# Query projection with x as the fixed operand and wq moving in 512 columns, in a one-token attention and MLP kernel

## Chip, cores, metric

One core of one Trainium2 chip (eight cores on two dies). The metric is the device time of one execution in microseconds, taken as the median of several runs. A profiled execution's span (first to last instruction) is about 1.9 us shorter than its time.

## The reference, cut to what matters

Two batch rows of one token, width 448. After a layer norm, 16 query heads of 256 attend to the last 4096 positions of 8 key and value heads, and an MLP runs beside it; all three are summed.

```python
q = (xn @ wq)                      # [2,448] @ [448,4096]
k, v = k_cache[:, :, Sk - 4096:], v_cache[:, :, Sk - 4096:]   # 2 x 8 heads x 4096 x 256, bf16
o = softmax(q k^T / 16) v
out = x + o @ wo + mish_mlp(xn)    # w1 448x1792, w2 1792x448
```

k and v are 33.6 MB each, the weights 10.6 MB (wq, wo 3.67 each, w1 and w2 together 3.21): 77.7 MB must be read for 2 x 448 outputs.

One warning about correctness: with inputs this small the softmax is nearly flat, and the comparison with the reference passes even when the query is a constant. So the comparison does not prove that the new projection gives the right q.

## The kernel before

wq borrows one of two large buffers that later hold v. It lies there as 128 partitions x 7 slices x 2048 columns. The projection uses 128x128 blocks of wq as the fixed operand and x (4 columns) as the moving one. The result has to be copied four times along the partitions ("spread").

```python
wq_sb = v_tile()[:, 0 : NS * HW].rearrange("p (s n) -> p s n", s=NS)   # 1 of 2 v buffers
nc.sync.dma_start(out=wq_sb, in_=A_wq...)                              # 28 KB runs
...
def project():
    for hh in range(HH):
        for e in range(NE):
            for s in range(NS):                                        # 8 * 2 * 7 = 112
                nc.tensor.matmul(qT_ps[:, hh, e, :], lhsT=wq_v[:, s, hh, e, :],
                                 rhs=xs[:, s, :, :]..., start=(s == 0), stop=(s == NS - 1))
    nc.vector.tensor_copy(out=qT[:], in_=qT_ps...)
    for b4 in range(NB):                                               # 4 spread matmuls
        nc.tensor.matmul(qr_ps[:, b4, :], lhsT=spread[:, b4, :], rhs=qT[:], ...)
    nc.vector.tensor_copy(out=qrep..., in_=qr_ps[:])
# build_q(i): eight GpSimd copies qrep -> qdiag[i % 2], the fixed operand of the scores
# ... cut ...
load_k(0); load_dense(); project(); build_q(0); build_q(1); turn(0)    # turn: DVE transpose of k
for i in range(Hkv + 1):
    load_k(i + 1); load_v(i); load_wo(i)      # all on one DMA queue, in this order
    # per quarter: turn, scores (PE), exp (ACT), transpose of p (DVE)
    # then the MLP (once, i == 0), values(i - 1), output of head i - 2
```

k and v have two buffers each. A load is issued when the last reader of its buffer is done, so the issue times of the loads are where a slower engine could reach the DMA stream.

The softmax here doesn't subtract the row's maximum and nothing guards it: scores larger than these inputs give would overflow.

## Time and profile before

| | before |
|---|---|
| time, median of the first 3 runs | 190.34 us (190.32 to 190.46) |
| span of the profiled run | 188.4 us |
| read from HBM | 77.67 MB |
| rate from 60 to 100, and 100 to 140 us | 429, 430 GB/s |
| PE busy in those 80 us | 66.6 us (83%) |
| DVE busy in those 80 us | 48.2 us (60%) |

The rate is the same in both 40 us stretches, whatever the engines do; PE is the busiest engine and still has a sixth of its time free.

### The profile page before, as it was taken

To read this page: it belongs to the slowest core of one execution; us is meant where nothing else is said; L and a number is where in the kernel's file an instruction comes from. 1 tells how busy PE (TensorE), PEld (TensorE's weight loads), DVE (VectorE), ACT (ScalarE), POOL (GpSimd) and SP (SyncE) were. 2 spreads that over 40 slices of the span, in tenths; PEclk is the share of its full clock that TensorE was granted. 3 is DMA by queue.
4 is the path that set the end of the run, shared out by engine and by line. 5 is a ranking of instruction groups with operands and counts; after the bars stand their busy time and mean duration, and the time that the engine had idled before them with its cause. 6 is when DMAs were issued, how large, how long until landed. Compare 5 with 4: busy or idle time off the path is not lost.

```text
span 188.4 us, 2773 instructions
## 1 busy us (share of the span) xinstructions
PE 138.5 (74%) x1118; PEld 68.2 (36%) x1118; DVE 106.0 (56%) x155; ACT 41.4 (22%) x140; POOL 16.1 (9%) x74
## 2 busy tenths in 40 slices
PE   0143079935989679966996599947996699988963
PEld 0042023733434234423342234413442334433852
DVE  6901299059931993089704991099606993967201
ACT  3100004400440315012421224012421224124101
POOL 6004200300030002100030003000030000000000
PEclk9999999955999978999799969995899969999855
DMA  6999899999999999999999999999999999999990
GB/s 226 445 444 428 383 432 438 445 442 440 431 431 438 445 407 404 433 438 398 462 447 431 431 431 438 414 418 420 449 431 431 412 423 435 473 418 386 427 375 23
DMA packets 5509, 77.82 MB, mean 413 GB/s; under 512 B 501, under 2 KB 2553, under 8 KB 2938
## 3 DMA queue, kind: packets, MB, share of 16 engines
q1 hardware_dynamic: 5492, 77.66, 96.8%
q8 instruction: 8, 0.13, 0.2%
q14 instruction: 3, 0.02, 0.0%
q10 hardware_dynamic: 6, 0.01, 0.0%
HBM read 77.67 MB, written 0.00 MB: 412 GB/s over the span
## 4 chain that ended last, share of the span: by engine, by line
DMA 67%; DVE 18%; PE 11%; ACT 1%; SPq 0%; issue 0%; ACTq 0%; DVEq 0%
DMA k<-in_A_k_cache_dram 58%; DVE kt L377 14%; DMA v<-in_A_v_cache_dram 10%; PE sc L389 6%; PE o L448 4%; DVE pT L415 3%; PE q L498 1%; PE psA L225 1%; ACT p L403 1%; DVE oT L462 0%; DVE sums L424 0%; SPq L353 0%; DVE osum L483 0%; SPq L111 0%; ACTq L595 0%
## 5 line engine op out<-in xcount | busy, mean ns | idle before, releaser
L377 DVE STREAM_TRANSPOSE kt<-k 128x2048 f32<-128x2048 f32 x32 | 73.1, 2289 | 57.0 <-DMA k<-in_A_k_cache_dram 57.0
L389 PE MATMUL sc<-kt,qdiag 128*128 128x512 bf16 x256 | 71.1, 437 | 19.7 <-DVE kt L377 19.6
L403 ACT ACTIVATE p<-sc,off 128x256 bf16<-128x256 f32 x64 | 33.0, 544 | 84.2 <-PE sc L389 83.5
L389 PEld LDWEIGHTS <-qdiag 128*128 128x128 bf16 x256 | 26.3, 107 | 61.1 <-issue 35.6
L448 PE MATMUL o<-v,pT 128*8 128x512 bf16 x192 | 42.5, 379 | 0.0
L448 PEld LDWEIGHTS <-pT 128*8 128x8 bf16 x192 | 17.2, 92 | 22.4
L272 POOL COPY qdiag<-qrep 32x16 bf16<-32x16 bf16 x64 | 13.0, 247 | 121.8 <-PE sc L389 107.4
L415 DVE STREAM_TRANSPOSE pT<-p 128x512 bf16<-128x512 bf16 x32 | 21.6, 677 | 2.8 <-ACT p L403 2.8
L403 ACT ACTIVATION_READ_ACCUMULATOR p<-sc,off 128x1 f32 x64 | 11.7, 183 | 0.0
L456 ACT COPY o_sb<-o 8x512 f32<-8x512 f32 x6 | 3.4, 574 | 36.3 <-PE o L448 36.3
L225 PE MATMUL psA<-wo,oT 128*2 128x112 bf16 x128 | 3.6, 238 | 8.9 <-DVE oT L462 8.9
L498 PE MATMUL q<-pT,v 128*128 128x4 bf16 x256 | 7.4, 168 | 1.9 <-DMA v<-in_A_v_cache_dram 1.8
L498 PEld LDWEIGHTS <-v 128*128 128x128 bf16 x256 | 7.2, 100 | 2.1 <-DMA v<-in_A_v_cache_dram 1.9
L246 PE MATMUL qT_ps<-xs,v 128*128 128x4 bf16 x112 | 3.1, 166 | 6.0 <-DMA v<-in_A_wq_dram 6.0
L225 PEld LDWEIGHTS <-oT 128*2 128x2 bf16 x128 | 1.8, 87 | 9.8 <-DVE oT L462 9.6
L246 PEld LDWEIGHTS <-v 128*128 128x128 bf16 x112 | 3.1, 104 | 6.2 <-DMA v<-in_A_wq_dram 6.2
L225 PE MATMUL psA<-v,act_bf 128*2 128x112 bf16 x56 | 1.5, 296 | 5.0 <-DVE act_bf L335 5.0
L188 PE MATMUL xnT_ps<-ident,xn_bf 2*128 2x2 bf16 x7 | 0.5, 167 | 5.4 <-DVE xn_bf L138 5.4
L479 PEld LDWEIGHTS q<-ident_f,o_sb 8*128 8x128 f32 x24 | 3.3, 206 | 3.0 <-issue 3.0
L462 DVE TENSOR_TENSOR oT<-q,rec 128x8 bf16<-128x8 f32 x2 | 0.3, 167 | 6.9 <-PE q L498 6.9
L479 PE MATMUL q<-ident_f,o_sb 8*128 8x8 f32 x24 | 3.8, 264 | 0.0
L303 PE MATMUL hT_ps<-xs,v 128*128 128x4 bf16 x49 | 3.7, 195 | 0.0
(55 smaller groups left out, 39.7 us busy)
## 6 DMA issues: line engine op xcount, KB each, us to landing
k<-in_A_k_cache_dram SPq DMA_DIRECT2D x7, 4096.0 KB, 29.7
v<-in_A_v_cache_dram SPq DMA_DIRECT2D x7, 4096.0 KB, 30.1
k<-in_A_k_cache_dram SPq DMA_DIRECT2D x2, 2048.0 KB
v<-in_A_wq_dram SPq DMA_DIRECT2D x1, 3584.0 KB
v<-in_B_w_dram SPq DMA_DIRECT2D x2, 1568.0 KB, 25.9
wo<-in_A_wo_dram SPq DMA_DIRECT2D x7, 448.0 KB, 29.7
v<-in_A_v_cache_dram SPq DMA_DIRECT2D x1, 2048.0 KB, 15.0
v<-in_A_v_cache_dram SPq DMA_DIRECT2D x1, 1536.0 KB, 18.1
```

The lines of the kernel that those rows point to most:

```text
L225: nc.tensor.matmul(part(n), lhsT=lhsT, rhs=w[:, n * DO : (n + 1) * DO], start=start, stop=stop, tile_position=(0, n * Q), skip_group_check ...
L246: nc.tensor.matmul(qT_ps[:, hh, e, :], lhsT=wq_v[:, s, hh, e, :], rhs=xs[:, s, :, :].rearrange("p x b -> p (x b)"), start=(s == 0), stop=( ...
L272: nc.gpsimd.tensor_copy(out=tv[rows, :, e, j * Q : (j + 1) * Q : HS].rearrange("p n (b h) -> p n b h", b=Bsz), in_=qrep[rows, :, h0 : h0 + ...
L303: nc.tensor.matmul(hT_ps[:, c, :, :].rearrange("p x b -> p (x b)"), lhsT=w1_v[:, s, c, :], rhs=xs[:, s, :, :].rearrange("p x b -> p (x b)" ...
L377: nc.vector.transpose(out=kt[:].bitcast(FP32), in_=k[:, half * TH * Dh : (half + 1) * TH * Dh].bitcast(FP32),)
L389: nc.tensor.matmul(psc[:], lhsT=qdiag[i % NW][:, n * NE + e, :], rhs=ktv[:, n, e, :, :], start=(n == 0 and e == 0), stop=(n == NB - 1 and ...
L403: nc.scalar.activation(out=pv[:, b, :, :], in_=sv[:, b, :, :], func=ACT.Exp, scale=scale, bias=off[:, b : b + 1], accum_out=state["rs", i] ...
L415: nc.vector.transpose(out=pT[:], in_=p_t.pop(s)[:])
L448: nc.tensor.matmul(po[:], lhsT=pT_t[i * NH + piece][:, uh * NP * Q : (uh + 1) * NP * Q : HS], rhs=v[:, u * NP : (u + 1) * NP, :].rearrange ...
L456: nc.scalar.copy(out=o_sb[:], in_=po[:])
L479: nc.tensor.transpose(pqv[:, u, c, :], ov[:, u, c, :], ident_f[0:NR, 0:NR])
L498: nc.tensor.matmul(po[:, c, :], lhsT=vv[:, t, c, :], rhs=pTv[:, th, 0:Q:HS], start=(t == 0 and c == 0), stop=(t == T - 1), skip_group_chec ...
```

## The change

The intent: x becomes the fixed operand (already repeated in four groups of 32 columns, so the spread step falls away), wq streams through in 512 columns, 28 matmuls in place of 112 and 4, and wq comes in two loads, so that PE can start after the first four of seven slices. A 32x32 transpose on DVE then puts q on the partitions.

```diff
-    nc.sync.dma_start(out=wq_sb, in_=A_wq...)
+    SC = NS // 2 + 1
+    for lo, hi in ((0, SC), (SC, NS)):
+        nc.sync.dma_start(out=wq_sb[:, lo:hi, :], in_=wq_in[:, lo:hi, :])
...
-    spread = consts.tile([P, NB, P], BF16)        # memset and 16 small DVE copies
...
     def project():
-        (112 matmuls wq x xs, cast, 4 spread matmuls, cast to qrep)
+        nc.vector.tensor_copy(out=xq[:, :, :, 0:NXB], in_=xs...to_broadcast([P, NS, NQ, NXB]))
+        pools = (ps_sc, "sc"), (ps_sc, "sc"), (ps_o, "o"), (ps_o, "o")
+        ps = [pool.tile([P, N5], FP32, tag=tag, name="q_ps") for pool, tag in pools]
+        for s in range(NS):
+            for u in range(4):
+                nc.tensor.matmul(ps[u][:], lhsT=xq[:, s, :, :]..., 
+                                 rhs=wq_sb[:, s, u * N5 : (u + 1) * N5], ...)
+        for u in range(4):                        # DVE, ACT, DVE, ACT
+            copy(out=q_sb[:, u * N5 : (u + 1) * N5], in_=ps[u][:])
+        nc.vector.transpose(out=qt[:].bitcast(FP32), in_=q_sb[:, 0:HW].bitcast(FP32))
...
     # build_q reads qt instead of qrep
```

More of the change, by code (lines that the diff above doesn't have):

```diff
@@ L110 @@
     wq_sb = v_tile()[:, 0 : NS * HW].rearrange("p (s n) -> p s n", s=NS)
-    nc.sync.dma_start(
-        out=wq_sb,
-        in_=A_wq.rearrange("r (x n) -> (r x) n", x=NX).rearrange("(p s) n -> p s n", s=NS),
-    )
+    wq_in = A_wq.rearrange("r (x n) -> (r x) n", x=NX).rearrange("(p s) n -> p s n", s=NS)
+    SC = NS // 2 + 1
+    for lo, hi in ((0, SC), (SC, NS)):
+        nc.sync.dma_start(out=wq_sb[:, lo:hi, :], in_=wq_in[:, lo:hi, :])
     make_identity(nc, ident[:])
@@ L149 @@
         )
-    spread = consts.tile([P, NB, P], BF16)
-    nc.gpsimd.memset(spread[:], 0.0)
-    for b4 in range(NB):
-        rows = slice(b4 * Q, (b4 + 1) * Q)
-        for j in range(NQ):
-            nc.vector.tensor_copy(
-                out=spread[rows, b4, j * Q : (j + 1) * Q], in_=ident[rows, rows]
-            )
     hsel = hsel[:, 0:BR]
@@ L235 @@
     add(ident[0:Bsz, 0:Bsz], x_bf[:, :], start=True)
-    qrep = consts.tile([P, NB, HH, NE, NX, Bsz], BF16)
-    wq_v = wq_sb.rearrange("p s (h m e) -> p s h e m", h=HH, e=NE)
-    def project():
-        qT_ps = ps_m.tile([P, HH, NE, NX * Bsz], FP32, tag="m", name="qT_ps")
-        for hh in range(HH):
-            for e in range(NE):
-                for s in range(NS):
-                    nc.tensor.matmul(
-                        qT_ps[:, hh, e, :],
-                        lhsT=wq_v[:, s, hh, e, :],
-                        rhs=xs[:, s, :, :].rearrange("p x b -> p (x b)"),
-                        start=(s == 0),
-                        stop=(s == NS - 1),
-                    )
-        n = HH * NE * NX * Bsz
-        qT = consts.tile([P, n], BF16, name="qT")
-        nc.vector.tensor_copy(out=qT[:], in_=qT_ps[:].rearrange("p h e c -> p (h e c)"))
-        qr_ps = ps_m.tile([P, NB, n], FP32, tag="m", name="qr_ps")
-        for b4 in range(NB):
-            nc.tensor.matmul(
-                qr_ps[:, b4, :], lhsT=spread[:, b4, :], rhs=qT[:], start=True, stop=True
-            )
+    xq = consts.tile([P, NS, NQ, Q], BF16)
@@ L261, in project @@
+    nc.gpsimd.memset(xq[:], 0.0)
+    NXB = NX * Bsz
+    qt = consts.tile([P, HW], BF16)
+    qv = qt[:].rearrange("p (h n k e) -> p n h k e", h=HH, n=NB, e=NE)
+    def project():
         nc.vector.tensor_copy(
-            out=qrep[:].rearrange("p n h e x b -> p n (h e x b)"), in_=qr_ps[:]
-        )
+            out=xq[:, :, :, 0:NXB],
+            in_=xs[:].rearrange("p s x b -> p s (x b)").unsqueeze(2).to_broadcast([P, NS, NQ, NXB]),
+        )
+        N5 = HW // 4
+        pools = (ps_sc, "sc"), (ps_sc, "sc"), (ps_o, "o"), (ps_o, "o")
+        ps = [pool.tile([P, N5], FP32, tag=tag, name="q_ps") for pool, tag in pools]
+        for s in range(NS):
+            for u in range(4):
+                nc.tensor.matmul(
+                    ps[u][:],
+                    lhsT=xq[:, s, :, :].rearrange("p j k -> p (j k)"),
+                    rhs=wq_sb[:, s, u * N5 : (u + 1) * N5],
+                    start=(s == 0),
+                    stop=(s == NS - 1),
+                )
+        q_sb = kt_pool.tile([P, TH * Dh], BF16, tag="kt", name="q_sb")
+        for u in range(4):
+            copy = nc.vector.tensor_copy if u % 2 == 0 else nc.scalar.copy
+            copy(out=q_sb[:, u * N5 : (u + 1) * N5], in_=ps[u][:])
+        nc.vector.transpose(out=qt[:].bitcast(FP32), in_=q_sb[:, 0:HW].bitcast(FP32))
@@ L275, in build_q @@
                     ),
-                    in_=qrep[rows, :, h0 : h0 + rep, e, x, :].rearrange("p n h b -> p n b h"),
+                    in_=qv[rows, :, h0 : h0 + rep, x * Bsz : (x + 1) * Bsz, e].rearrange(
+                        "p n h b -> p n b h"
+                    ),
                 )
```

## The prediction

> **What bounds the kernel now.** I read the page's busy shares first, then the chain that ended last, the DMA rows in 40 slices, the queue of DMA issues in order of time, the first 36 us in order of time, and the busy time and GB/s in short windows.
>
> Busy shares: PE 74%, DVE 56%, ACT 22%, POOL 9%. The DMA rows say something else (each digit is the mean busy share of the 16 DMA engines in 1/40 of the span, 4.71 us; below it the rate):
>
> ```profile
> DMA  6999899999999999999999999999999999999990
> GB/s 226 445 444 428 383 432 438 445 442 440 431 431 438 445 407 404 433 438 398 462 447 431 431 431 438 414 418 420 449 431 431 412 423 435 473 418 386 427 375 23
> DMA packets 5509, 77.82 MB, mean 413 GB/s; under 512 B 501, under 2 KB 2553, under 8 KB 2938
> ...
> DMA 67%; DVE 18%; PE 11%; ACT 1%; SPq 0%; issue 0%; ACTq 0%; DVEq 0%
> ```
>
> From the second slice to the last but one the transfers never pause. The first slice moved 226 x 4.71 = 1.06 MB, some 2.4 us worth, so they start at about 2.3 us; the last data of v release PE at 182.75 us. 77.7 MB in 180.4 us is 431 GB/s. So the time is a head of 2.3 us, a stream of 180.4 us and a tail of 188.4 - 182.75 = 5.7 us. The stream is the bound. The chain's 67% for DMA understates it: where the chain passes through DVE or PE (as at 22.5 to 32.5 us, before the issue of the third k load) the rows above show that the DMA engines were busy with earlier loads.
>
> The projection lies in the head (start us, us, engine, line, operation):
>
> ```profile
> 5.42 1.61 DVE L155 COPY spread<-ident 32x32 bf16<-32x32 bf16 x16
> ...
> 12.09 3.15 PE L246 MATMUL qT_ps<-xs,v 128*128 128x4 bf16 x112 [6.03 <-DMA v<-in_A_wq_dram]
> ...
> 15.27 0.54 SPq L353 DMA_DIRECT2D v<-in_A_v_cache_dram  x1
> 15.27 0.22 DVE L255 CAST qT<-qT_ps 128x64 bf16<-128x64 f32 x1 [5.96 <-PE qT_ps L246]
> ...
> 15.96 0.42 DVE L261 CAST qrep<-qr_ps 128x256 bf16<-128x256 f32 x1 [0.46 <-PE qr_ps L258]
> 16.53 3.52 POOL L272 COPY qdiag<-qrep 32x16 bf16<-32x16 bf16 x16 [12.83 <-DVE qrep L261]
> ...
> 22.54 6.70 DVE L377 STREAM_TRANSPOSE kt<-k 128x2048 f32<-128x2048 f32 x3 [6.16 <-DMA k<-in_A_k_cache_dram]
> 24.90 9.92 PE L389 MATMUL sc<-kt,qdiag 128*128 128x512 bf16 x32 [8.98 <-DVE kt L377]
> ```
>
> PE waits until 12.09 for all of wq, projects in 3.15 us, and its end releases wq's buffer to the first v load (issued 15.27). The first block of qdiag is complete at 18.17 us (PE's first weight load from it), yet the scores start only at 24.90, because k lands at 22.54 and its transpose ends at 24.86. The query is thus ready almost 7 us early.
>
> How early the loads are issued, from the DMA queue in order of time:
>
> ```profile
> 2.96 0.55 SPq L353 DMA_DIRECT2D k<-in_A_k_cache_dram  x1
> 15.27 0.54 SPq L353 DMA_DIRECT2D v<-in_A_v_cache_dram  x1
> 15.85 0.60 SPq L370 DMA_DIRECT2D wo<-in_A_wo_dram  x1
> 32.55 0.54 SPq L353 DMA_DIRECT2D k<-in_A_k_cache_dram  x1
> 45.82 0.54 SPq L353 DMA_DIRECT2D v<-in_A_v_cache_dram  x1
> ```
>
> Bytes moved, summed from 5 us windows: 3.3 MB by 10 us, 7.8 by 20, 12.1 by 30, 14.2 by 35, 18.4 by 45, 22.8 by 55. Bytes submitted before the first v: wq 3.67 + k 4.19 + w1 and w2 3.21 + second k 4.19 = 15.27 MB, which the stream has used up at 37.5 us; so that v has 22 us to spare. The third k (issued 32.55) would be missed when 19.92 MB are through, at about 48.5 us: 16 us to spare. The second v (45.82) would be missed at 24.12 MB, about 58 us: 12 us to spare. Those are the three issues that a slower projection can push.
>
> **What the Trainium skill says.** "DMA: Bandwidth & Descriptors", Specifications, gives a fabric ceiling of 435 GB/s for the core's 16 engines; the trace's 431 GB/s over the stream agrees that there is nothing left to fill. The same table asks for runs of at least 512 B for line rate; wq's runs go from 28 KB to 16 and 12 KB, so I expect no loss (the trace has 28, 32 and 12.5 KB runs side by side at 428 to 445 GB/s). "Queues, rings and completion order" of that page says each engine consumes descriptors in ring order: the first piece of wq should land before the second, and neither later. "TensorE: Matmul & The Clock Gate", Part 1, says an idle array runs at half rate until some 3.4 us of sustained work, and gives 426.7 and 215.7 ns for 512 columns. The trace agrees in size: the first eight score matmuls take 3.59 us (449 ns each), their weight loads are 0.43 us apart from 24.91 to 30.41 us, and the 32 value matmuls at 54.8 us take 7.08 us (221 ns). The clock row reads full speed before 30 us although these matmuls are slow, so I trust durations there, not that row.
>
> **The change part by part.**
>
> Removed: 112 matmuls of 4 columns (3.15 us, 112 weight loads of 104 ns beside them), four spread matmuls (0.37), the casts qT and qrep (0.22 + 0.42), 16 small copies to spread (1.61 us of DVE before xs), and spread's memset (0.52 on POOL).
>
> Added: 28 matmuls of 512 columns; a broadcast copy xs to xq (estimate 0.25 us from the 0.22 us of the xs instructions); a memset of xq (128x896; the 128x1024 one takes 0.95, so 0.85 us, done by about 4 us on POOL); four evictions of 128x512, two on DVE and two on ACT; one DVE transpose of 128x1024 words; one more DMA issue (0.4 us of SP). In the order of instructions the loads, scores and transposes after the projection are unmoved; q's scratch takes one turn in the kt buffers, but the fifth k transpose still waits for the same scores.
>
> Start: xs was done at 9.3 us; without the spread copies 7.7, xq at 8.0. The first piece of wq is 2.10 MB, through at 5 + 0.81/0.402 = 7.0 us; all of wq was through at about 10.8 and released PE at 12.09, a lag of 1.3. So the first piece releases PE at 8.3 us, 3.8 us earlier.
>
> Matmuls: PE is cold. With 5.5 us of half rate as in the scores, some 13 cost 0.427 (to 13.8 us), the other 15 cost 0.221 (3.3 us): end at 17.2 us. If it stays cold, 28 x 0.427 = 12.0 us: end at 20.3. By then the second piece (12.1 us) has long landed, so PE doesn't wait for it. Compared with 15.24 the projection ends 2 to 5 us LATER in spite of its earlier start: its PE time grows from 3.15 to between 9 and 12 us.
>
> Behind it: evictions. The casts of 64 and 256 columns took 0.224 and 0.424 us, 1.04 ns a column, so 0.69 us for 512; two on DVE, of which the first starts 0.65 us before PE's end: done 0.75 us after it. ACT's 8x512 copy took 0.574, so ACT is done sooner. Transpose: half of the 2.29 us of 128x2048, 1.15 to 1.2 us. So qt stands 2.0 us after PE's end (before, qrep stood 1.14 us after): 19.2, or 22.3 cold. First qdiag, 8 x 0.22 = 1.76 us: 21.0, or 24.1.
>
> On the path: the scores wait for the k transpose, which starts at 22.54 with k's landing. DVE is free for it in both cases (19.2 or 22.3), and qdiag is there before 24.86. Change of the first scores, and of the third k issue: 0 us, at worst 0.5. The first v issue moves from 15.27 to between 17.3 and 20.4, against 37.5 that it may have. Stream: same bytes, same order; 128 more runs and one more completion, which I put at 0 to 0.2 us. Tail: untouched. Sum: 0 to +0.2 us on 190.34.
>
> **Rivals.**
> 1. The late projection starves the stream. For: PE work triples and q is later. Against: 12 to 22 us of backlog at each issue concerned, against a shift of at most 5. It would need q to be 10 us later than I reckon; then each further us costs one: 192 to 196.
> 2. The shorter projection path helps, as the change intends. For: PE starts 3.8 us earlier, and PE may be warm for the scores (cold matmuls there cost 14 x 0.21 = 3 us). Against: the k transpose waits for k's landing, which is the stream; earlier work can't bring bytes sooner. It would give 190.0 to 190.3 at best.
> 3. The split load changes the stream itself: smaller runs slower, or the dip at 19 to 24 us (383 GB/s) removed or made worse. A dip to 383 instead of 431 in one slice costs 0.5 us, so +-0.5: 189.8 to 190.9.
> 4. Another PE clock phase in the tail (64 matmuls in 1.87 us and 0.7 us for the output, at granted clock 0.50): a warm tail could take off up to about 1 us. The work from 165 us on is unchanged, so it should stay cold.
>
> **Range and chances.** The centre is 190.4. Rivals 3 and 4 and the scatter of before (0.14 us) give 189.7 to 191.1 for 8 in 10. The 2% bounds lie at 186.5 and 194.1. Faster needs less data, a faster stream than the 431 it has, or a tail shortened by two thirds: 0.01. Slower needs rival 1 or a broken stream: 0.03. Within 2%: 0.96.
>
> **What would show it.** Right: the mean of the DMA rows stays at 9 throughout with some 430 GB/s, the projection's first matmul at about 8.3 us and its last at 17 to 20.5, the first k transpose still at 22.5, scores at 24.9, the last v released at about 182.7, tail 5.7. PE busy grows by 5 to 9 us with no effect. Wrong: a slice of low DMA share between 35 and 60 us (rival 1), the first k transpose held back by qt rather than k's landing by more than 1 us, or a stream that ends at a clearly different time with the same bytes (rival 3).

## The result

| | before | changed |
|---|---|---|
| time, median of 6 runs each | 190.40 us (190.06 to 191.11) | 190.16 us (189.86 to 190.75) |
| ratio, 95% interval | | 0.9988 (0.9966 to 1.001): same |
| span of the profiled run | 188.4 us | 188.0 us |
| PE busy | 138.5 us | 140.3 us |
| rate from 60 to 100, and 100 to 140 us | 429, 430 GB/s | 429, 429 GB/s |

A ratio is the mean time of one kernel's runs over that of the other's of the same rounds, so it is not quite the ratio of the medians quoted.

The DMA rows of the changed kernel's page, and its chain by engine, answer to the first block of the prediction:

```profile
DMA  6999899999999999999999999999999999999991
GB/s 220 421 476 439 383 426 439 446 443 446 432 439 436 399 404 435 439 439 394 474 441 439 418 404 429 432 446 413 452 446 422 398 425 422 457 439 411 411 385 38
...
DMA 67%; DVE 19%; PE 11%; SPq 1%; ACT 1%; issue 0%; ACTq 0%; DVEq 0%
```

The same shape as before, down to the 383 in the fifth slice. That dip is thus not caused by the single wq load, and it is not removed by the split.

The changed kernel in order of time (start us, us, engine, line, operation, tiles, count, in brackets the idle time before and its releaser):

```profile
8.08 0.21 DVE L237 COPY xq<-xs 128x112 bf16<-128x112 bf16 x1
8.35 8.81 PE L246 MATMUL q_ps<-v,xq 128*128 128x512 bf16 x28 [1.97 <-DVE xq L237]
...
13.45 0.15 PEld L246 LDWEIGHTS <-xq 128*128 128x128 bf16 x1 [0.28 <-issue]
13.76 2.90 PEld L246 LDWEIGHTS <-xq 128*128 128x128 bf16 x14 [0.17 <-issue]
16.55 1.29 DVE L256 CAST q_sb<-q_ps 128x512 bf16<-128x512 f32 x2 [8.26 <-PE q_ps L246]
...
17.19 0.54 SPq L349 DMA_DIRECT2D v<-in_A_v_cache_dram  x1
...
17.94 1.25 DVE L257 STREAM_TRANSPOSE qt<-q_sb 128x1024 f32<-128x1024 f32 x1
19.34 3.53 POOL L266 COPY qdiag<-qt 32x16 bf16<-32x16 bf16 x16 [15.31 <-DVE qt L257]
20.97 0.10 PEld L385 LDWEIGHTS <-qdiag 128*128 128x128 bf16 x1 [4.30 <-POOL qdiag L266]
21.57 6.70 DVE L373 STREAM_TRANSPOSE kt<-k 128x2048 f32<-128x2048 f32 x3 [2.38 <-DMA k<-in_A_k_cache_dram]
23.93 7.00 PE L385 MATMUL sc<-kt,qdiag 128*128 128x512 bf16 x24 [6.77 <-DVE kt L373]
```

The projection starts 3.7 us earlier (8.35 against 12.09) and ends 1.9 us later (17.16 against 15.24). The weight loads stay 0.43 us apart until 13.45 us: PE is cold for 13 matmuls, as reckoned from the score matmuls of before. The query's first block is complete at 20.97 us instead of 18.17. Still the scores wait 3 us more for the k transpose, and that waits for k's landing.

Three later issues on the DMA queue of the changed kernel, which answer to the last block of the prediction:

```profile
31.54 0.54 SPq L349 DMA_DIRECT2D k<-in_A_k_cache_dram  x1
46.08 0.54 SPq L349 DMA_DIRECT2D v<-in_A_v_cache_dram  x1
46.66 0.59 SPq L366 DMA_DIRECT2D wo<-in_A_wo_dram  x1
```

The third k comes 1 us sooner than before (k landed 1 us sooner in this execution), the second v 0.3 us later. Neither reaches the stream, whose queue is full at both times. By 60 us the windows add up to 25.1 MB in the changed kernel and 25.0 in the one before, by 100 us to 42.3 and 42.2, by 140 us to 59.4 in both.

### The profile page after: what moved, and what is told of

It is laid out like the page before. It is cut to its first block, busy times and chain, and to the rows that moved or that the text cites. A ratio compares the mean times of both kernels' runs of the same rounds, so it can differ in the third digit from the quotient of the medians.

```text
span 188.0 us, 2587 instructions
## 1 busy us (share of the span) xinstructions
PE 140.3 (75%) x1030; PEld 67.3 (36%) x1030; DVE 106.6 (57%) x141; ACT 42.5 (23%) x142; POOL 16.4 (9%) x74
## 4 chain that ended last, share of the span: by engine, by line
DMA 67%; DVE 19%; PE 11%; SPq 1%; ACT 1%; issue 0%; ACTq 0%; DVEq 0%
DMA k<-in_A_k_cache_dram 57%; DVE kt L373 14%; DMA v<-in_A_v_cache_dram 10%; PE sc L385 6%; PE o L444 4%; DVE pT L411 3%; PE q L494 1%; ACT p L399 1%; PE psA L217 1%; SPq L114 0%; DVE oT L458 0%; DVE sums L420 0%; SPq L349 0%; DVE osum L479 0%; ACTq L591 0%
## 5 line engine op out<-in xcount | busy, mean ns | idle before, releaser
L385 PE MATMUL sc<-kt,qdiag 128*128 128x512 bf16 x256 | 68.1, 421 | 19.1 <-DVE kt L373 18.1
L385 PEld LDWEIGHTS <-qdiag 128*128 128x128 bf16 x256 | 25.5, 105 | 59.0 <-issue 27.1
L444 PEld LDWEIGHTS <-pT 128*8 128x8 bf16 x192 | 17.2, 92 | 22.4
L266 POOL COPY qdiag<-qt 32x16 bf16<-32x16 bf16 x64 | 13.0, 248 | 120.7 <-PE sc L385 103.8
L411 DVE STREAM_TRANSPOSE pT<-p 128x512 bf16<-128x512 bf16 x32 | 21.5, 673 | 2.5 <-ACT p L399 2.4
L246 PE MATMUL q_ps<-v,xq 128*128 128x512 bf16 x28 | 8.8, 491 | 2.0 <-DVE xq L237 2.0
L494 PEld LDWEIGHTS <-v 128*128 128x128 bf16 x256 | 7.4, 101 | 2.3 <-DMA v<-in_A_v_cache_dram 1.7
L256 DVE CAST q_sb<-q_ps 128x512 bf16<-128x512 f32 x2 | 1.3, 684 | 8.3 <-PE q_ps L246 8.3
L246 PEld LDWEIGHTS <-xq 128*128 128x128 bf16 x28 | 3.3, 121 | 7.2 <-issue 3.5
```

Source lines behind the costliest of these rows:

```text
L246: nc.tensor.matmul(ps[u][:], lhsT=xq[:, s, :, :].rearrange("p j k -> p (j k)"), rhs=wq_sb[:, s, u * N5 : (u + 1) * N5], start=(s == 0), st ...
L256: copy(out=q_sb[:, u * N5 : (u + 1) * N5], in_=ps[u][:])
L266: nc.gpsimd.tensor_copy(out=tv[rows, :, e, j * Q : (j + 1) * Q : HS].rearrange("p n (b h) -> p n b h", b=Bsz), in_=qv[rows, :, h0 : h0 + r ...
L385: nc.tensor.matmul(psc[:], lhsT=qdiag[i % NW][:, n * NE + e, :], rhs=ktv[:, n, e, :, :], start=(n == 0 and e == 0), stop=(n == NB - 1 and ...
L411: nc.vector.transpose(out=pT[:], in_=p_t.pop(s)[:])
L444: nc.tensor.matmul(po[:], lhsT=pT_t[i * NH + piece][:, uh * NP * Q : (uh + 1) * NP * Q : HS], rhs=v[:, u * NP : (u + 1) * NP, :].rearrange ...
```

## The experiments

The theory: the stream of loads sets the time; the projection lies beside it, with 12 to 22 us to spare at the issues it can push. The rivals: the query is on the path (then each us of it counts), or the split load changes the stream.

### One part at a time: e1_split_only, e2_proj_only

e1: the kernel before with the two-piece load.

```diff
-    nc.sync.dma_start(out=wq_sb, in_=A_wq...)
+    for lo, hi in ((0, SC), (SC, NS)):
+        nc.sync.dma_start(out=wq_sb[:, lo:hi, :], in_=wq_in[:, lo:hi, :])
```

> The old projection with wq in two loads. Stream theory (the loads bound the time, the projection lies beside them): same time as before within 0.3 us, 190.1 to 190.7; projection still starts at about 12.1 us because its first column group needs all seven slices of wq. Rival 3 (the split itself changes the stream): the first k lands at about 21.5 us as in the changed kernel instead of 22.5, and the time moves by up to 0.5 us either way. If k lands at 22.5 here, the 1 us earlier landing seen in the changed kernel is not from the split.

Measured: 190.34 us (189.74 to 190.58) against 190.42, ratio 0.9992 (0.9978 to 1.0005). The first k transpose started at 22.97 us, so the landing at 21.57 in the changed kernel is not from the split. One detail of the expectation was off: four matmuls of the first group (slices 0 to 3) did run at 9.46 us; the rest waited until 12.37. Rival 3 has no support here.

e2: the changed kernel with wq in one load (the diff above, reversed).

> The new projection with wq in one load. It can start only when all of wq has landed, about 12.1 us; 28 matmuls take 8.8 us as in the changed kernel, so they end at about 20.9, the q transpose at about 23.0 (2.0 us later), the first k transpose starts at about 23.0 instead of 22.5 and the third k is issued 0.5 to 1 us later than before. Stream theory: none of it shows, 190.1 to 190.7. The theory that the query is on the path: 0.5 us or more slower than before, some 1.5 us slower than the changed kernel.

Measured: 189.95 us (189.82 to 190.30), ratio 0.9981 (0.9968 to 0.9994). In order of time, the run without the split (same columns as above):

```profile
12.15 7.71 PE L246 MATMUL q_ps<-v,xq 128*128 128x512 bf16 x28 [5.78 <-DMA v<-in_A_wq_dram]
...
20.64 1.25 DVE L257 STREAM_TRANSPOSE qt<-q_sb 128x1024 f32<-128x1024 f32 x1
21.81 6.67 DVE L373 STREAM_TRANSPOSE kt<-k 128x2048 f32<-128x2048 f32 x3
24.15 7.03 PE L385 MATMUL sc<-kt,qdiag 128*128 128x512 bf16 x21 [4.29 <-DVE kt L373]
```

The matmuls took 7.71 us, not 8.8 (fewer of them cold), so the expected delay shrank: the transpose of q ends just when the k transpose starts. The query is 2.7 us later than in the changed kernel, and the time is not longer: the query is not on the path. The time even lies 0.15 us below the stated range of 190.1 to 190.7; these tenths are taken up below.

### The two ends: no projection work, no wq at all

e3 keeps the wq load but replaces the matmuls and evictions by a constant (wrong); e4 drops the load as well.

```diff
-        for s in range(NS): for u in range(4): nc.tensor.matmul(ps[u][:], ...)
-        for u in range(4): copy(out=q_sb[...], in_=ps[u][:])
+        nc.vector.memset(q_sb[:, 0:HW], 0.01)
```

> Wrong result on purpose: wq is loaded, but no projection matmuls or evictions; q is a constant, ready before 10 us. This is the most that any faster projection could bring. Stream theory: 190.0 to 190.5, no gain beyond 0.2 us; first scores still wait for the k transpose. Projection-on-path theory: the time falls by the projection's 2 to 5 us.

Measured: 190.91 us (190.27 to 190.95), ratio 1.0019 (1.0007 to 1.0031). The first v was issued at 11.92 us, the first scores ran at 23.91, as in the changed kernel. With no projection at all nothing is won; it is even 0.4 us above the stated range. The profile shows where the extra time may lie: PE stands still for 0.9 us before the last 7 matmuls on v, which start at 185.15 us, while in the changed kernel all of them are done by 184.26. In the kept trace a 16 KB packet of the instruction queue (q8 on the page) ends 1.5 us before that start, at 183.66, so PE may have waited for its own instructions. This is read off one trace and not tested. Even with the whole 0.9 us taken off, an estimate, 190.0 us would remain, so ending the projection sooner is worth 0.4 us at most.

> Wrong result on purpose: as the kernel without matmuls, and wq isn't loaded at all, so 3.67 MB of 77.67 less. Stream theory: time falls by 3.67 MB at 431 GB/s = 8.5 us, to about 181.8 (181.0 to 182.6). If something else than the stream sets the time (compute per head), it falls by clearly less than 8 us.

Measured: 181.90 us (181.73 to 182.31), ratio 0.9557 (0.9545 to 0.9569). The bytes line of its page:

```profile
HBM read 74.00 MB, written 0.00 MB: 411 GB/s over the span
```

3.67 MB less and 0.0443 x 190.42 = 8.4 us less: 3.67 / 8.4 = 437 GB/s, the rate of the stream within 2%. Against e3, which differs from e4 only in the load, it is 0.0462 x 190.42 = 8.8 us, or 417 GB/s, within 3%. The time follows the bytes, not the work.

### How late may the query be: the matmuls two, four and six times

The accumulation is simply repeated, with the same result.

```diff
+        for _ in range(2):          # 4, 6
             for s in range(NS):
                 for u in range(4): nc.tensor.matmul(ps[u][:], ...)
```

> The changed kernel with the projection's 28 matmuls done twice (same result). They end at 17.2 + 6.2 = 23.4 us, first scores at about 27 us (3 us late), third k issued at about 34.7. Stream theory: all within the backlog, 190.0 to 190.6. If the query were on the path: +3 us, 193.

> Projection done four times: it ends at about 35.8 us, so the first v is issued at about 36 us, against 37.5 us at which the loads submitted before it run out; scores start at about 39.5, third k issued at about 47, against 48.5. Stream theory: just at the edge, 190.2 to 193. A theory without a backlog (each us of projection costs a us) says +18.6 us, 208.

> Projection done six times: it ends at about 48.2 us. Now the first v comes too late: the loads submitted run out at 37.5 us and the first v starts to move at about 50, so the DMA rows show a gap of some 12 to 13 us there and the time rises to about 203 (200 to 207). If there is no gap and no rise, the backlog is larger than I reckon; if the rise is 31 us, there is no backlog.

| run | projection ends | first v issued | first scores | time | ratio to before |
|---|---|---|---|---|---|
| changed | 17.2 us | 17.2 us | 23.9 us | 190.16 us | 0.9988 |
| e5, twice | 22.9 us | 22.9 us | 27.1 us | 189.86 us | 0.9965 (0.9952 to 0.9978) |
| e6, four times | 34.6 us | 34.6 us | 38.9 us | 191.05 us | 1.0028 (1.001 to 1.0045) |
| e7, six times | 46.5 us | 46.5 us | 50.8 us | 203.28 us | 1.067 (1.0646 to 1.0694) |

Six times the matmuls, DMA rows of the page (each slice is 5.03 us here):

```profile
DMA  6999899405998999999999999999999999999990
GB/s 228 424 489 424 374 470 417 215 0 209 417 394 378 417 378 408 457 430 432 427 417 443 430 432 424 427 437 443 424 430 420 437 404 430 456 437 397 422 363 20
```

And the same run in short windows (span of the window, us, busy us of PE, weight loads, DVE, ACT, POOL, granted clock, DMA share, GB/s):

```profile
35.00:37.00 2.00, 2.00 (x11) 0.88 (x9) 0.00 (x0) 0.00 (x0) 0.00 (x0) 1.00 1.06 459
37.00:38.00 1.00, 1.00 (x6) 0.48 (x5) 0.00 (x0) 0.00 (x0) 0.00 (x0) 1.00 0.31 131
38.00:40.00 2.00, 2.00 (x10) 0.89 (x10) 0.00 (x0) 0.00 (x0) 0.00 (x0) 1.00 0.04 16
40.00:45.00 5.00, 4.95 (x24) 2.25 (x23) 0.00 (x0) 0.00 (x0) 0.00 (x0) 1.00 0.00 0
45.00:47.00 2.00, 1.49 (x7) 0.48 (x5) 1.12 (x2) 0.91 (x2) 0.00 (x0) 1.00 0.00 0
47.00:49.00 2.00, 0.00 (x0) 0.00 (x0) 1.90 (x3) 1.45 (x2) 0.33 (x2) 1.00 0.89 262
```

The stream runs dry in the 38th microsecond, where the sum of the submitted bytes had put it (37.5 us), stands still until 47 us, and moves again in the window after the late issue at 46.5. This is what a starved stream looks like; neither kernel of the comparison has it. The gap is some 10 us, a little less than the 12 to 13 expected, chiefly because the projection ended at 46.5 and not at 48.2. It fills the three low slices: (430 - 215 + 430 + 430 - 209) x 5.03 us = 4.4 MB, or 10 us at 430 GB/s; the six slices after it run at 378 to 417 and miss another 0.9 MB, some 2 us. Together that is some 12.3 of the 12.8 us of the result. A likely reason for the lower rate afterwards, read off and not tested, is that the next two loads come just in time as well: the third k is issued at 58.41 us, when the 19.92 MB submitted before it are nearly through (18.4 MB by 55 us, 20.3 by 60), and the second v at 68.39 us, when the 24.12 MB are.

Four times is near the edge, as expected, and the time rises by 0.5 us. The profile does not show a gap before the first v, though. Its window from 37 to 38 us falls to 295 GB/s, but so does that of e1 and of e3, and the changed kernel has 246 there. What differs is that e6 has moved 24.6 MB by 60 us, against 25.0 and 25.1 in the two kernels. It falls behind between 50 and 55 us (401 GB/s against 466 in the changed kernel), after its third k, which was issued at 46.01 us, 2.5 us before the reckoned edge of 48.5. Whether that issue is the cause was not tested.

Doubling the projection costs nothing, although it moves the first scores by 3.2 us and the third k to 34.64 us. At 189.86 us it lies 0.14 us below the stated range.

### More pieces: e8_seven_loads

```diff
-    for lo, hi in ((0, SC), (SC, NS)):
+    for lo, hi in ((i, i + 1) for i in range(NS)):
```

> wq in seven loads of 4 KB runs instead of two: five more completions and 640 more runs, and 2.3 us more of issuing before the first k is submitted. Stream theory: 190.0 to 190.6. Rival 3 (smaller runs or more completions slow the stream): an effect larger than that of the two loads, 0.5 us or more slower. The projection can't start before xq at about 8.3 us, so it ends at 17.2 as with two loads.

Measured: 190.76 us (189.80 to 190.88) against 190.47, ratio 0.9999 (0.9981 to 1.0017). The first k was submitted at 4.83 us instead of 1.65, and the windows add up to 24.6 MB by 60 us instead of 25.1. So seven pieces do put the stream some 0.5 MB behind at the start, which should cost 1 us; a cost of that size isn't seen in the ratio. No effect of two pieces can be read from this. Three details of the expectation were off: the median lies 0.16 us above its range, the first k was delayed by 3.2 us and not 2.3, and the projection ended at 16.2 us and not 17.2.

### The last tenths: x1_late_v_pe, x2_late_v_dve, e9_tail_cuts, e10_late_and_tail

Without e4, e6 and e7 the runs so far differed by up to 0.5%, and the times seemed to order by the issue of the first v. Two edits of the kernel before delay only that issue: x1 by idle matmuls on wq, x2 by one tiny copy that reads wq's buffer after the first k transpose.

```diff
 x1, after the cast to qrep in project():
+        for _ in range(20):
+            nc.tensor.matmul(idle_ps[:], lhsT=spread[:, 0, :],
+                             rhs=wq_sb[:, NS - 1, 0 : HW // 4], start=True, stop=True)
 x2, after turn(0):
+    late = consts.tile([1, 1], BF16)
+    nc.vector.tensor_copy(out=late[:], in_=wq_sb[0:1, 0, 0:1])
```

> So far the time orders by when the first v is issued: 190.9 at 11.9 us (no matmuls), 190.4 at 15.3 (before), 190.2 at 17.2 (changed), 189.95 at 19.9 (projection only), 189.9 at 22.9 (projection twice). This run is the kernel before with 20 idle matmuls of 512 columns on wq behind the true projection: the query is as early as before, the first v is issued at about 23 us. Theory A (a later first issue of v, or the PE work up to then, is worth 0.3 to 0.5 us): 189.8 to 190.1. Theory B (scatter between builds, no effect of the issue): 190.3 to 190.6.

> The kernel before, with one 1x1 copy on DVE that reads wq's buffer after the first k transpose, so that the first v is issued at about 24.9 us with no work added on PE. Theory A, issue time: 189.8 to 190.1. Theory A, PE work: 190.3 to 190.6, as before. Theory B: 190.3 to 190.6.

Measured: x1 190.02 us (189.88 to 190.65), ratio 0.9982 (0.9967 to 0.9998), first v issued at 22.03 us; x2 190.54 us (190.24 to 190.77), ratio 1.0000 (0.9985 to 1.0014), first v issued at 25.05 us. x2 gives the issue time of v, which I had taken for the order of the runs, no support as a cause: its interval leaves at most a gain of 0.15%, where 0.3 to 0.5 us are 0.16 to 0.26%. PE work ahead of the scores fits e2, e5 and x1 (faster by 0.2 to 0.35%) and e3 (none, slower by 0.2%). It is neither shown nor excluded: e8, e9 and e10 have the changed kernel's PE work and came out at 0.9993 to 1.0001, with intervals that overlap the changed kernel's. What makes these tenths stays open.

e9 cuts the last v load finer, to shorten what follows the last landing; e10 has both e9's cuts and x2's copy on top of the changed kernel.

```diff
-            load_v(i, ... (0, T // 2, 7 * T // 8, T))
+            load_v(i, ... (0, T // 2, 3 * T // 4, 7 * T // 8, T))
```

> The changed kernel with the last v load cut at 1/2, 3/4, 7/8 instead of 1/2, 7/8. The 64 matmuls behind the last landing become 32 or fewer (1.87 us to about 0.9), but the last output matmuls also need the last wo loads, which land at about 184.3 us. Head + stream + tail theory: the tail shrinks by 0.1 to 0.5 us, so 189.7 to 190.1; this is the only part outside the stream that I can shorten.

> The changed kernel with both: first v issued at about 24 us by a 1x1 copy on DVE, and the finer cuts of the last v. If the two small effects are real and add: 189.5 to 189.8. If neither: 190.0 to 190.4, as the changed kernel.

Measured: e9 190.31 us (190.10 to 190.52), ratio 0.9993 (0.998 to 1.0007); e10 190.44 us (190.18 to 190.89), ratio 1.0001 (0.9987 to 1.0016). e9 missed its range. e10 shows no sum of two effects; it lies at the upper end of the range for "neither". The end of e9 (first block) and of the changed kernel (second), in order of time:

```profile
183.85 1.08 PE L494 MATMUL q<-pT,v 128*128 128x4 bf16 x35 [1.52 <-issue]
185.18 0.54 PE L217 MATMUL psA<-wo,oT 128*2 128x112 bf16 x16 [0.26 <-DVE oT L458]
```

```profile
182.33 1.93 PE L494 MATMUL q<-pT,v 128*128 128x4 bf16 x64 [1.58 <-DMA v<-in_A_v_cache_dram]
184.51 0.59 PE L217 MATMUL psA<-wo,oT 128*2 128x112 bf16 x16 [0.26 <-DVE oT L458]
```

With finer cuts PE has fewer matmuls left (35) but starts them later, at 183.85 us; the page names no releaser there. As in e3, a 16 KB packet of the instruction queue ends shortly before, at 182.58 us (in e10, which has the same pause, at 182.38), so this wait too may be for instructions, and it may have taken the gain of the finer cuts. That was not tested. In the changed kernel the very last piece of v lands some 18.8 us after its issue at about 164.8, at 183.6, while PE is still busy with the piece before. Of the 64 matmuls only the last 16 use that piece, so most of them were hidden behind the last bytes already. No combination that I ran is shown to beat the changed kernel: e5 has the lowest median, but it wasn't run beside the changed kernel, and what makes it so is open.

## Why the prediction was right

**Bound.** Right: 429 to 430 GB/s in both 40 us stretches in both kernels, the same bytes by 60, 100 and 140 us, and e4's 8.4 us for 3.67 MB.

**Start of the projection.** Predicted 8.3 us from the load, measured 8.35, but set by xq (8.08 + 0.21 us, where 8.0 was reckoned). That the two agree to 0.05 us is partly luck. The load was hardly earlier: where xq was ready sooner, PE waited for the first piece of wq, until 8.13 us in e5, 8.39 in e6 and 8.21 in e7. Dropping the spread copies was what made xq this early.

**Its duration and end.** Predicted 17.2 us (20.3 if all cold), measured 17.16: 13 matmuls at 0.43 us, then the fast ones. The five profiled builds with one pass of these 28 matmuls took 7.71 to 8.81 us, because between some 7 and 13 of them were slow. So the hit to 0.04 us is luck; such a figure is good to about a microsecond.

**Evictions, transpose, qdiag.** Predicted q ready at 19.2, first qdiag 21.0; measured 19.19 and 20.97. The transpose took 1.25 us against 1.15 to 1.2, the DVE casts 0.684 each against 0.69.

**Path.** Right: the k transpose waited for k, not for q. The first k transpose moved to 21.57 from 22.54, which I had not foreseen; it starts between 21.5 and 23.1 us over the runs that don't delay it, early in builds with the new projection (e2, e3, e9, e10) and late in those with the old (e1, x1, x2). e8, the new one with seven loads, is late too, at 22.68. The time doesn't follow it.

**Sum.** 190.4 predicted, 190.16 measured; a change of 0 to +0.2 us predicted, -0.2 +- 0.4 measured.

**PE busy.** I said 5 to 9 us more; the page shows 1.8 more. The projection itself grew by 5.3 us (8.8 against 3.1 and 0.4), but the score matmuls shrank from 71.1 to 68.1 us as more of them ran at the fast rate. That line varies between 63.1 and 72.2 us over the profiled builds. The step that failed is adding a difference on one line to a total that also depends on the clock's state.

**Rival 1** (starvation) is real but some 17 us of delay away (first v at 17.2 us, the edge in e6 at 34.6): it appears in e7 at the place that the bytes submitted give, and e6 is 0.5 us slower near that edge. **Rival 2** fails on e3. **Rival 3** has no support in e1. **Rival 4**: the granted clock in the last 4 us was 0.50 in both kernels.

One reading of mine was imprecise: I took 182.75 us for the end of the stream. That is the landing of the last piece but one; the last of v lands at about 183.6 in the changed kernel and wo after it, so the stream is nearer to 182 us and the tail nearer to 4. The sum isn't changed by it, but it misled me in e9.

## What to carry to other kernels

Before judging a faster compute step at the start of a kernel that streams its data, add up the bytes submitted before each load that the step can delay, and compare with the bytes moved: the difference over the rate is the time by which that load may slip for free, less about 1 us between an issue and its first bytes (46.5 and after 47.5 us in e7). A step inside it is worth nothing, faster or slower, to within the 0.35% that stayed unexplained here. Check that sum with a kernel that does the step several times; the DMA rows must stay full up to the reckoned point and break there. And when only bytes set the time, test that by leaving bytes out, not work.

## What the Trainium skill lacked or had wrong

- "DMA: Bandwidth & Descriptors", Specifications, lists 358 GB/s as the HBM limit of a core beside the fabric's 435. This core, alone, read 429 to 430 GB/s from 60 to 140 us. "HBM Reference", Specifications (TRN2), has it right: a core alone measures about 425. The first table misleads only if read alone; its page says further down that a core gets the 358 when both cores of a pair stream.
- "TensorE: Matmul & The Clock Gate", Part 1, puts the change to the fast rate at around 4 us, give or take 0.5 us from run to run, and says that the number of slow matmuls varies. Here 13 matmuls were slow, 5.4 us (8.35 to 13.76), and the same 28 matmuls took 7.71, 7.84, 8.17, 8.30 and 8.81 us in five builds: the slow stretch lasted between some 3 us (e2) and 5.4 us, a wider spread than the page's.
- The same page warns that clock events are not reliable. A case that fits: the granted clock reads 1.00 from 5 to 15 us in the changed kernel, while the weight loads are 0.43 us apart.
- No page gives a measured duration for a DVE transpose of 32-bit words in 32x32 blocks. Measured: 1.245 us for 128x1024, 2.29 us for 128x2048.
